# Attention and a feed-forward layer on one core: transposes, second products and the last output in another order

## The chip, the core and the metric

The kernel runs on one core of a Trainium2 chip. A core has five engines with instruction streams of their own: TensorE (PE in the profile; its weight loads are shown apart as PEld), VectorE (DVE), ScalarE (ACT), GpSimd (POOL) and SyncE (SP), which here only issues transfers. They wait for each other by semaphores. Transfers run on 16 DMA engines; what SP issues goes through a hardware queue, what GpSimd issues through a software queue. The metric is the time of one execution on the device, in microseconds (us); lower is better.

## The reference

Inputs are q, k, v of shape (4 batches, 8 heads, 768 positions, 64) in fp32, a decay lam for each head, and two weight matrices. Decayed linear attention comes first, then a feed-forward layer with an ELU:

```python
for b in range(nb):                     # blocks of 64 positions
    intra = np.einsum('bhic,bhjc->bhij', qb, kb) * Dmask[None]
    intra = np.einsum('bhij,bhjd->bhid', intra, vb)
    inter = np.einsum('bhid,bhde->bhie', qb * lam_pow[None], kv_state)
    out[:, :, sl] = intra + inter
    kv_state = lam_block[None, :, None, None] * kv_state + np.einsum('bhsd,bhse->bhde', kb_dec, vb)
...
h = x @ w_in                            # 3072 x 512 by 512 x 2048
g = np.where(h > 0.0, h, alpha * (np.exp(np.minimum(h, 0.0)) - 1.0))
return (g @ w_out).astype(np.float32)   # 3072 x 2048 by 2048 x 512
```

## The kernel before

The kernel takes blocks of 128 positions. Chunk g is one such block of one batch: batch g mod 4, block g div 4, 24 chunks in all. Every chunk goes through the attention and then through the feed-forward layer, and the stages of different chunks are interleaved by hand.

An order list of tokens is run one after the other; each token emits its instructions on all engines, and every engine keeps the order in which they were emitted. The first part of the list (`OPEN`, lines 51 to 59) is written by hand and reaches to the middle of chunk 6's and 7's second products; the rest is made by a rule (lines 575 to 612) that puts every other token at a fixed distance from the first products. The tokens are:

- `L12`: loads q, k, v of chunks 12 and 13 (three transfers that also cast to fp16, issued by GpSimd, line 107). From chunk 4 on chunks are loaded in pairs.
- `W9`: from chunk 8 on, issues the two transposing transfers of chunk 9 on SP (`qT`, `kT`, line 266), then on GpSimd `kd` = k times a decay (line 172) and the two products `stt` of the old state with the block's decay (line 376). The `stt` wait for the state of four chunks earlier. `T5` does the transposes of the first chunks on TensorE instead.
- `S8:9`: the score matmuls of chunks 8 and 9 on TensorE (line 300, into banks A, B and C, D of PSUM), and on VectorE four products `pp` with the causal mask (line 316); two of these at once, the others one by one with later tokens (the list `late`).
- `B:P8:P9:U8:U9`: the burst for both chunks: output of the attention (lines 336 and 342), its copy `xt` (line 359), and the new state (lines 404 and 416).
- `1:8:3`: part 3 of the first product for the pair that begins at chunk 8 (line 476, eight matmuls of 256 columns into one of the two buffers `psH`), then on ScalarE an exponential `e` (line 482) and a ReLU in place (line 483). VectorE's `g`, which combines them (line 455), is emitted with the next product token (`flush`), and only then is the `psH` buffer free.
- `2:6:3`: quarter 3 of the second product of chunk 6 (line 498, four matmuls of 512 columns that add to `psM`, of which there are two banks, M0 and M1). After quarter 3, ScalarE copies `psM` to `osb` (line 513; four buffers of 512 columns), and SP stores it (line 448); `mm1` emits all stores but the newest.

The last token is `2:23:3`, with `last` set: its four matmuls are done for columns 0 to 255 and again for 256 to 511, both in the same bank. VectorE copies the first half (line 511), ScalarE the second. `emit_stores` at the end emits what is left.

The part of the list that the change touches, with the rule's part behind the last line of `OPEN`:

```
S8:9 1:6:2 1:6:3 2:4:3 2:5:3 L12 1:6:4 B:P8:P9:U8:U9 1:6:5 W11 1:6:6 2:6:0 2:6:1 W10 1:6:7 2:6:2
1:8:0 S10:11 1:8:1 1:8:2 2:6:3 1:8:3 W12 2:7:0 1:8:4 B:P10:P11:U10:U11 2:7:1 1:8:5 W13 2:7:2 1:8:6
```

Of the kernel before, what the change touches and what calls it, by code (L numbers as in the profile page):

```python
# [7 lines left out]
FP32 = mybir.dt.float32  # L8
FP16 = mybir.dt.float16
# [6 lines left out]
def kernel(  # L16
# [11 lines left out]
    nc = tc.nc  # L28

    B, H, S, D = q.shape  # L30
    L = 128
    NHP = H // 2
    DM = H * D
    DFF = moe_w_in.shape[1]
    NFT = DFF // 128
    NCB = S // L
    NG = B * NCB
    FB = 4
    NJ = NFT // FB
    GPE = 8  # L40
    GSIZE = {**{g: 1 for g in range(4)}, **{g: 2 for g in range(4, NG, 2)}}
    GFIRST = {g0 + i: g0 for g0, n in GSIZE.items() for i in range(n)}
    WI = [2] * 8
# [15 lines left out]
    )  # L59
    LAGU = 7  # L60
    AT = {"L": -18, "W": -13, "T": -9, "S": -8, "B": -4}
# [10 lines left out]
    asb = ctx.enter_context(tc.tile_pool(name="asb", bufs=1))  # L72
    msb = ctx.enter_context(tc.tile_pool(name="msb", bufs=1))
    ps = ctx.enter_context(tc.tile_pool(name="ps", bufs=1, space=bass.MemoryType.PSUM))
# [45 lines left out]
    def cast_raw(g, w, eng):  # L120
        n = f"{w}{g}"
        t = asb.tile([128, 1, H, 64], FP16, tag=f"{w}n1", name=f"{w}n{g}", bufs=4)
        (qg if w == "q" else kg)[g] = t
        if eng == 0:
            nc.vector.tensor_copy(t[:, 0], raw[n][:])
        else:
            nc.scalar.copy(t[:, 0], raw[n][:])

    def of(tiles, g):
        g0, i = group_of[g]  # L130
        return tiles[g0][:, i]

    wi16, wo16, wi_of, wo_of = [], [], {}, {}
# [113 lines left out]
    def bank(what, i, shape, dtype, name):  # L247
        tag = TAGS[what].split()[i]
        return ps.tile(
            shape, dtype, tag=f"ps{tag}", name=name, bufs=2 if tag == "H" else 1  # L250
        )
# [10 lines left out]
    def att_T_dma(g):  # L262
        ts = []
        for w, tiles in (("q", qg), ("k", kg)):
            t = asb.tile([128, NHP, 128], FP16, tag=f"{w}T", name=f"{w}T{g}", bufs=5)
            nc.sync.dma_start_transpose(
                out=t[:], in_=of(tiles, g).rearrange("p h d -> p (h d)")
            )
            ts.append(t)
        qkT[g] = ts  # L270

    def att_T_pe(g):
        n = len(TAGS[f"T{g}"].split())
        pts = [
            bank(f"T{g}", i, [128, 2 // n, NHP, 128], FP16, f"psT{g}_{i}")
            for i in range(n)
        ]
        pts = [pts[0][:, 0], pts[n - 1][:, 2 // n - 1]]
        for src, pt in zip((of(qg, g), of(kg, g)), pts):
            for hp in range(NHP):  # L280
                nc.tensor.transpose(  # L281
                    pt[:, hp, :], in_=src[:, 2 * hp : 2 * hp + 2, :], identity=ident16[:]
                )
        qt, kt = [
            asb.tile([128, NHP, 128], FP16, tag=f"{w}T", name=f"{w}T{g}", bufs=5)
            for w in "qk"
        ]
        nc.vector.tensor_tensor(out=qt[:], in0=pts[0], in1=qs[:], op=ALU.mult)
        nc.scalar.copy(out=kt[:], in_=pts[1])
        qkT[g] = (qt, kt)  # L290
# [34 lines left out]
    def att_P(g):  # L325
# [21 lines left out]
        def evacuate():  # L347
            g0 = GFIRST[g]
            n = GSIZE[g0]
            if g0 not in xg:  # L350
# [4 lines left out]
            dst = xg[g0][:, :, (g - g0) * 128 : (g - g0 + 1) * 128]  # L355
            if g < GPE:
                nc.scalar.copy(out=dst, in_=po[:])  # L357
# [85 lines left out]
    gts, psM, stores, pending = {}, {}, [], []  # L443

    def emit_stores(keep=0):
        while len(stores) > keep:
            dst, o = stores.pop(0)
            nc.sync.dma_start(out=dst, in_=o)

    def flush():  # L450
        while pending:
            g0, j, e, r = pending.pop(0)
            n = GSIZE[g0]
            g = msb.tile([128, FB // n, n, 128], FP16, tag="g", bufs=40, name=f"g{g0}_{j}")
            nc.vector.scalar_tensor_tensor(  # L455
                out=g[:].rearrange("p f c t -> p (f c t)"), in0=e[:], scalar=-1.0, in1=r[:],
                op0=ALU.add, op1=ALU.min,
            )
            for f in range(FB // n):
                for c in range(n):  # L460
                    gts[(g0 + c, j * (FB // n) + f)] = g[:, f, c, :]
        if late:
            late.pop(0)()

    def mm1(g0, j):
        flush()
        emit_stores(1)
        n = GSIZE[g0]
        assert {f"P{g0 + i}" for i in range(n)} <= seen
# [15 lines left out]

    mm2_done = {g: 0 for g in range(NG)}

    def mm2(g, j, last=False):
        flush()
        if mm2_done[g] == 0:  # L490
            psM[g] = bank(f"M{g}", 0, [128, DM], FP32, f"psM{g}")
        first, mm2_done[g] = mm2_done[g] == 0, mm2_done[g] + 1
        end = mm2_done[g] == NJ
        halves = [slice(0, DM // 2), slice(DM // 2, DM)] if last else [slice(0, DM)]
        for hi, cols in enumerate(halves):
            for f in range(FB):
                i, w = wo_of[j * FB + f]
                nc.tensor.matmul(  # L498
                    psM[g][:, cols], lhsT=gts[(g, j * FB + f)], rhs=wo16[i][:, w, cols],
                    start=first and f == 0, stop=end and f == FB - 1, skip_group_check=True,  # L500
                )
            if end:
                out_of(g, cols, nc.vector if last and hi == 0 else nc.scalar)

    def out_of(g, cols, eng):
        cb, b = divmod(g, B)
        t0 = b * S + cb * L
        w = cols.stop - cols.start
        o = msb.tile([128, w], FP32, tag=f"osb{w}", bufs=4, name=f"osb{g}_{cols.start}")
        if eng is nc.vector:  # L510
            eng.tensor_copy(o[:], psM[g][:, cols])
        else:
            eng.copy(o[:], psM[g][:, cols])  # L513
        stores.append((out[t0 : t0 + 128, cols], o[:]))

    def zero_st(b):
        nc.scalar.memzero(st[b][0][:])
# [5 lines left out]
    def pool_work(g):  # L523
        if g >= GPE:
            att_T_dma(g)
        att_kd(g)
        att_M(g)
# [3 lines left out]
    def ready(t):  # L531

        g = int(t[1:])
        if t[0] == "P":
            assert g < B or f"U{g - B}" in seen
        if t[0] == "U" and g < 2 * B:
            assert f"{'z' if g < B else 'Z'}{g % B}" in seen
        if t[0] == "U" and g >= B:
            assert f"U{g - B}" in seen and (g < 2 * B or f"P{g - B}" in seen)
        seen.add(t)  # L540

    def run(t):
        w, *a = t[0], *t[1:].replace(":", " ").split()
        if w == "B":
            for o in a:
                ready(o)
            burst(*a)
            return
        a = [int(x) for x in a]
        if w in "PUzZ":  # L550
            ready(t)
        if w == "S":
            for g in a:
                att_S(g)
            for g in a:
                late.extend(att_E(g))
            late.pop(0)()
            late.pop(0)()
        elif w == "P":
            burst(t)  # L560
        elif w == "U":
            late.extend(att_U(*a))
            while late:
                late.pop(0)()
        else:
            {"T": att_T_pe, "1": mm1, "2": mm2, "Z": zero_st, "z": zero_st1,
             "q": lambda g, e: cast_raw(g, "q", e), "k": lambda g, e: cast_raw(g, "k", e),
             "c": lambda i: (emit_qs, emit_mask, emit_ks)[i](), "W": pool_work, "L": load_pair,
             "M": next_M, "w": zero_matmuls}[w](*a)

    for t in FIRST.split():
# [3 lines left out]
    prog = OPEN.split()  # L575
    done = set(prog) | {o for t in prog if t[0] == "B" for o in t.split(":")}
    m1 = [(g, j) for g, n in GSIZE.items() for j in range(NJ * n)]
    place = {u: i for i, u in enumerate(m1)}
    need = {
        (g, j): place[(GFIRST[g], ((j + 1) * FB - 1) // (FB // GSIZE[GFIRST[g]]))]  # L580
        for g in range(NG) for j in range(NJ)
# [3 lines left out]
    for g in range(0, NG, 2):  # L585
        u = place[(GFIRST[g], 0)] - (8 if GSIZE[GFIRST[g]] == 4 and g == GFIRST[g] else 0)
        for t, p in (
# [4 lines left out]
            h = int(t[1:].replace(":", " ").split()[0].strip("P"))  # L592
            if t[0] == "W" and h < 8 or t[0] == "L" and h < 12 or t[0] == "T" and h >= GPE or t in done:
                continue
# [4 lines left out]
    first = place[m1[0]]  # L599
# [10 lines left out]
            n -= 1  # L610
    for g, j in m2:
        prog.append(f"2:{g}:{j}")
    prog[-1] += ":1"
    for t in prog:
        run(t)
    while late:
        late.pop(0)()
    emit_stores()
# [30 lines left out]
```

## Time and profile before

| what | us |
|---|---|
| median of 3 runs | 216.61 |
| lowest and highest of the 3 | 215.79, 217.13 |
| the profiled execution, its own time | 217.26 |
| its span, first to last instruction | 215.5 |
| first products, L476: 896 matmuls, busy | 99.3 |
| second products, L498: 388 matmuls, busy | 96.4 |
| `g` on VectorE, L455: 96 of 0.686 | 65.8 |
| ScalarE's `e` and ReLU, L482 and L483: 96 each of about 0.6 | 57.3 and 57.0 |
| store of 256 KB (`out_dram<-osb`), issue to landing, median | 2.3 |
| transposes `qT` and `kT`, issue to landing, median | 3.9 and 2.8 |
| loads of q, k, v in pairs, issue to landing, median | 7.0, 8.3, 8.6 |

A row of the profile names the line and engine, the operation, what it writes and reads, the shape, the number of instructions, the busy time and the mean time of one; behind the bar or in square brackets stands the idle time of the engine just before, and what ended it. In a row of the order in time the first two numbers are the start from the span's beginning and the length. TensorE's granted clock was 0.997 of full speed on the mean. Because matmuls are pipelined, a group's shown length has its drain in it, and the next group can start before the shown end.

### The profile page before, as it was taken

How to read it: one execution, taken by the hardware profiler on the slowest of the kernel's cores; microseconds unless marked ns; L12 is line 12 of the kernel's file. 1: busy time of each engine (PE TensorE's matmuls, PEld its weight loads, DVE VectorE, ACT ScalarE, POOL GpSimd, SP SyncE). 2: the span in 40 equal slices, each digit the busy share in tenths (PEclk: the TensorE clock that was granted, in tenths of full speed). 3: DMA queues.
4: the chain of work that ended last, by engine and by line, in shares of the span. 5: the costliest groups of instructions: out<-in, count | busy, mean ns of one | idle time of the engine just before them, and what ended most of it. 6: DMA issues, size and time to landing. Idle time of an engine off the chain costs nothing.

```text
span 215.5 us, 5132 instructions
## 1 busy us (share of the span) xinstructions
PE 203.4 (94%) x2054; PEld 137.8 (64%) x2054; DVE 130.1 (60%) x224; ACT 129.1 (60%) x245; POOL 96.1 (45%) x115
## 2 busy tenths in 40 slices
PE   7767899999999998999999999999999999999992
PEld 2455577768685775766766766766766666766641
DVE  3936363787837788658657667667567456544410
ACT  4545565874776656565565566476476576566720
POOL 7996991999996419177167159300000000000000
PEclk9999999999999999999999999999999999999998
DMA  8999999999999957979939919999123110111021
GB/s 89 140 176 192 191 137 172 153 173 143 151 156 179 128 108 108 155 119 110 160 85 114 179 63 101 149 182 151 52 73 73 52 49 0 55 49 49 3 92 54
DMA packets 101977, 24.59 MB, mean 114 GB/s; under 512 B 92609, under 2 KB 99009, under 8 KB 101953
## 3 DMA queue, kind: packets, MB, share of 16 engines
q0 software_dynamic: 79760, 13.50, 83.1%
q1 hardware_dynamic: 22192, 10.76, 22.5%
q8 instruction: 16, 0.26, 0.5%
q14 instruction: 9, 0.07, 0.1%
HBM read 27.27 MB, written 6.29 MB: 156 GB/s over the span
## 4 chain that ended last, share of the span: by engine, by line
PE 83%; DMA 7%; POOL 6%; issue 1%; DVE 1%; ACT 0%; SPq 0%; POOLq 0%
PE psM L498 38%; PE psH L476 36%; DMA wo<-in_moe_w_out_dram 4%; DMA kT<-kn 3%; PE psO L336 3%; PE psS L300 3%; PE psO L342 2%; POOL wi L146 1%; POOL kn L107 1%; POOL vn L107 1%; POOL qn L107 1%; PE psT L281 1%; PE psU L404 1%; POOL kd L172 0%; POOL wo L153 0%
## 5 line engine op out<-in xcount | busy, mean ns | idle before, releaser
L476 PE MATMUL psH<-xt,wi 128*128 128x256 f16 (+1 forms) x896 | 99.3, 257 | 2.4 <-DMA wi<-in_moe_w_in_dram 0.9
L455 DVE SCALAR_TENSOR_TENSOR g<-e,psH 128x512 f16<-128x512 f32 x96 | 65.8, 686 | 57.6 <-ACT psH L483 56.8
L498 PE MATMUL psM<-wo,g 128*128 128x512 f16 (+1 forms) x388 | 96.4, 377 | 1.4 <-DMA wo<-in_moe_w_out_dram 0.9
L482 ACT ACTIVATE e<-psH 128x512 f32<-128x512 f32 x96 | 57.3, 597 | 66.4 <-PE psH L476 63.2
L476 PEld LDWEIGHTS <-wi 128*128 128x128 f16 x896 | 77.0, 98 | 27.7 <-DVE g L455 2.0
L483 ACT ACTIVATE psH<-psH 128x512 f32<-128x512 f32 x96 | 57.0, 594 | 0.0
L498 PEld LDWEIGHTS <-g 128*128 128x128 f16 x388 | 36.3, 98 | 30.4 <-issue 1.8
L316 DVE TENSOR_TENSOR pp<-psS,mask 128x512 f16<-128x512 f32 x48 | 30.9, 685 | 4.2 <-PE psS L300 4.2
L172 POOL TENSOR_TENSOR kd<-kn,ks 128x512 f16<-128x512 f16 x20 | 20.7, 1039 | 18.0 <-DMA kn<-in_k_dram 17.1
L376 POOL TENSOR_TENSOR stt<-st,upp 64x256 f32<-64x256 f16 x32 | 19.5, 608 | 19.2 <-DVE st L416 13.6
L513 ACT COPY osb<-psM 128x512 f32<-128x512 f32 (+1 forms) x24 | 13.9, 581 | 6.3 <-PE psM L498 6.3
L107 POOL DMA_DIRECT2D vn<-in_v_dram x14 | 15.5, 1109 | 1.9 <-DMA wi<-in_moe_w_in_dram 1.9
L107 POOL DMA_DIRECT2D kn<-in_k_dram x14 | 15.5, 1106 | 0.8 <-POOLq L633 0.8
L107 POOL DMA_DIRECT2D qn<-in_q_dram x13 | 14.8, 1139 | 0.0
L416 DVE TENSOR_TENSOR st<-stt,psU 64x256 f16<-64x256 f32 x32 | 13.3, 417 | 1.2 <-PE psU L404 0.5
L336 PE MATMUL psO<-pp,vn 128*64 128x128 f16 x192 | 12.0, 222 | 1.7 <-DMA vn<-in_v_dram 1.5
L359 DVE TENSOR_TENSOR xt<-psO,qs 128x512 f16<-128x512 f32 x16 | 11.0, 688 | 4.1 <-PE psO L342 4.1
L336 PEld LDWEIGHTS <-vn 128*64 128x64 f16 x192 | 9.7, 109 | 5.1 <-issue 2.9
L342 PE MATMUL psO<-qT,st 128*64 128x128 f16 x160 | 10.0, 219 | 0.0
L342 PEld LDWEIGHTS <-st 128*64 128x64 f16 x160 | 8.9, 110 | 0.0
L300 PE MATMUL psS<-qT,kT 64*128 64x128 f16 x192 | 8.1, 218 | 0.9 <-DMA kT<-kn 0.5
L357 ACT CAST xt<-psO 128x512 f16<-128x512 f32 x8 | 4.4, 588 | 6.9 <-PE psO L336 4.8
(41 smaller groups left out, 70.8 us busy)
## 6 DMA issues: line engine op xcount, KB each, us to landing
out_dram<-osb SPq DMA_DIRECT2D x23, 256.0 KB, 2.3
kn<-in_k_dram POOLq DMA_DIRECT2D x10, 256.0 KB, 8.3
qn<-in_q_dram POOLq DMA_DIRECT2D x10, 256.0 KB, 7.0
vn<-in_v_dram POOLq DMA_DIRECT2D x10, 256.0 KB, 8.6
wi<-in_moe_w_in_dram POOLq DMA_DIRECT2D x8, 256.0 KB, 6.9
wo<-in_moe_w_out_dram POOLq DMA_DIRECT2D x8, 256.0 KB, 7.9
kn<-in_k_dram POOLq DMA_DIRECT2D x4, 128.0 KB, 4.1
vn<-in_v_dram POOLq DMA_DIRECT2D x4, 128.0 KB, 5.9
```

The costliest lines, as they stand in the source:

```text
L107: nc.gpsimd.dma_start(out=t[:].rearrange("p b h d -> p (b h) d"), in_=src)
L172: nc.gpsimd.tensor_tensor(out=kd[:], in0=of(kg, g), in1=ks[:].unsqueeze(2).broadcast_to([128, H, 64]), op=ALU.mult,)
L300: nc.tensor.matmul(psS[g][hh][:, hp, :], lhsT=kt[r, hp, :], rhs=qt[r, hp, :], start=True, stop=True,)
L316: nc.vector.tensor_tensor(out=P[:], in0=pts[hh][:], in1=mask[:, hh::2, :], op=ALU.mult)
L336: nc.tensor.matmul(po[r, hp, :], lhsT=vt[:, 2 * hp + hh, :], rhs=Pt[(g, hh)][:, hp, :], start=True, stop=(cb == 0), skip_group_check=True,)
L342: nc.tensor.matmul(po[r, hp, :], lhsT=st[b][cb % 2][:, hp, r], rhs=qt[:, hp, :], start=False, stop=True, skip_group_check=True,)
L376: nc.gpsimd.tensor_tensor(out=tmp[r], in0=old[r, :, r], in1=upp[r].unsqueeze(2).broadcast_to([64, NHP, 64]), op=ALU.mult,)
L455: nc.vector.scalar_tensor_tensor(out=g[:].rearrange("p f c t -> p (f c t)"), in0=e[:], scalar=-1.0, in1=r[:], op0=ALU.add, op1=ALU.min,)
L476: nc.tensor.matmul(pH[:, f * n * 128 : (f + 1) * n * 128], lhsT=wi16[i][:, kk, w * 128 : (w + 1) * 128], rhs=xg[g0][:, kk, :], start=(kk = ...
L482: nc.scalar.activation(e[:], pH[:], AF.Exp)
L483: nc.scalar.activation(pH[:], pH[:], AF.Relu)
L498: nc.tensor.matmul(psM[g][:, cols], lhsT=gts[(g, j * FB + f)], rhs=wo16[i][:, w, cols], start=first and f == 0, stop=end and f == FB - 1, ...
```

## The change

A sixth buffer is given to `qT` and `kT`. In the hand-written list, `W11` and `W10` move ahead of `1:6:4` and `L12` moves behind `2:6:1`; the list goes on to `2:7:1`, with the second products `2:6:3`, `2:7:0` and `2:7:1` each placed ahead of `1:8:1`, `1:8:2` and `1:8:3`, and none of them between `1:8:3`, `1:8:4`, the burst of 10 and 11, and `1:8:5`. The last chunk's second product is made for columns 0 to 383 in its four tokens, and for columns 384 to 511 in a new function `mm2_rest` after them, in bank A. VectorE copies the first part, ScalarE the second, and each part's store is emitted at once.

```diff
+    LAST = NG - 1
+    CUT = 384
...
-        "2:4:2 S8:9 1:6:2 1:6:3 2:4:3 2:5:3 L12 1:6:4 B:P8:P9:U8:U9 1:6:5 W11 1:6:6 2:6:0 "
-        "2:6:1 W10 1:6:7 2:6:2"
+        "2:4:2 S8:9 1:6:2 1:6:3 2:4:3 2:5:3 W11 W10 1:6:4 B:P8:P9:U8:U9 1:6:5 1:6:6 2:6:0 "
+        "2:6:1 L12 1:6:7 2:6:2 1:8:0 S10:11 2:6:3 1:8:1 2:7:0 1:8:2 2:7:1"
...
-            t = asb.tile([128, NHP, 128], FP16, tag=f"{w}T", name=f"{w}T{g}", bufs=5)
+            t = asb.tile([128, NHP, 128], FP16, tag=f"{w}T", name=f"{w}T{g}", bufs=6)
...
-    def mm2(g, j, last=False):
+    def mm2(g, j):
         flush()
+        cols = slice(0, CUT if g == LAST else DM)
...
-        halves = [slice(0, DM // 2), slice(DM // 2, DM)] if last else [slice(0, DM)]
-        for hi, cols in enumerate(halves):
-            for f in range(FB):
-                i, w = wo_of[j * FB + f]
-                nc.tensor.matmul(
-                    psM[g][:, cols], lhsT=gts[(g, j * FB + f)], rhs=wo16[i][:, w, cols],
-                    start=first and f == 0, stop=end and f == FB - 1, skip_group_check=True,
-                )
-            if end:
-                out_of(g, cols, nc.vector if last and hi == 0 else nc.scalar)
+        for f in range(FB):
+            i, w = wo_of[j * FB + f]
+            nc.tensor.matmul(
+                psM[g][:, cols], lhsT=gts[(g, j * FB + f)], rhs=wo16[i][:, w, cols],
+                start=first and f == 0, stop=end and f == FB - 1, skip_group_check=True,
+            )
+        if end:
+            out_of(g, psM[g][:, cols], cols, nc.vector if g == LAST else nc.scalar)
+
+    def mm2_rest():
+        cols = slice(CUT, DM)
+        rest = ps.tile([128, DM - CUT], FP32, tag="psA", name="psMrest", bufs=1)
+        for f in range(NFT):
+            i, w = wo_of[f]
+            nc.tensor.matmul(
+                rest[:], lhsT=gts[(LAST, f)], rhs=wo16[i][:, w, cols],
+                start=f == 0, stop=f == NFT - 1,
+            )
+        out_of(LAST, rest[:], cols, nc.scalar)
...
         stores.append((out[t0 : t0 + 128, cols], o[:]))
+        if g == LAST:
+            emit_stores()
...
-    prog[-1] += ":1"
     for t in prog:
         run(t)
+    mm2_rest()
```

More of the change, by code (lines that the diff above doesn't have):

```diff
@@ L284, in att_T_pe @@
         qt, kt = [
-            asb.tile([128, NHP, 128], FP16, tag=f"{w}T", name=f"{w}T{g}", bufs=5)
+            asb.tile([128, NHP, 128], FP16, tag=f"{w}T", name=f"{w}T{g}", bufs=6)
             for w in "qk"
@@ L493, in mm2, with out_of @@
         end = mm2_done[g] == NJ
-        halves = [slice(0, DM // 2), slice(DM // 2, DM)] if last else [slice(0, DM)]
-        for hi, cols in enumerate(halves):
-            for f in range(FB):
-                i, w = wo_of[j * FB + f]
-                nc.tensor.matmul(
-                    psM[g][:, cols], lhsT=gts[(g, j * FB + f)], rhs=wo16[i][:, w, cols],
-                    start=first and f == 0, stop=end and f == FB - 1, skip_group_check=True,
-                )
-            if end:
-                out_of(g, cols, nc.vector if last and hi == 0 else nc.scalar)
-    def out_of(g, cols, eng):
+        for f in range(FB):
[16 more added lines that the diff above has]
+        out_of(LAST, rest[:], cols, nc.scalar)
+    def out_of(g, src, cols, eng):
         cb, b = divmod(g, B)
@@ L510, in out_of @@
         if eng is nc.vector:
-            eng.tensor_copy(o[:], psM[g][:, cols])
+            eng.tensor_copy(o[:], src)
         else:
-            eng.copy(o[:], psM[g][:, cols])
+            eng.copy(o[:], src)
         stores.append((out[t0 : t0 + 128, cols], o[:]))
+        if g == LAST:
+            emit_stores()
     def zero_st(b):
```

## The prediction

> **What bounds the kernel.** I read the page first, then busy time by stretches, then the order in time of TensorE, VectorE and the SP queue where TensorE stood still. The page:
>
> ```profile
> span 215.5 us, 5132 instructions
> ...
> PE 203.4 (94%) x2054; PEld 137.8 (64%) x2054; DVE 130.1 (60%) x224; ACT 129.1 (60%) x245; POOL 96.1 (45%) x115
> ...
> PE   7767899999999998999999999999999999999992
> ...
> PE 83%; DMA 7%; POOL 6%; issue 1%; DVE 1%; ACT 0%; SPq 0%; POOLq 0%
> ```
>
> TensorE is the bound. Its tenths are below 9 in the first five slices (before 27 us), in the one around 83 us, and at the end. The chain of waits adds a DMA share. An order change can win only where TensorE stands; the stretches say where that is past the start:
>
> ```profile
> 66.00:72.00 6.00, 5.49 (x56) 3.98 (x54) 5.16 (x10) 2.75 (x7) 4.24 (x7) 1.00 1.96 206
> ...
> 78.00:84.00 6.00, 5.74 (x52) 3.62 (x50) 5.06 (x10) 3.51 (x8) 3.95 (x6) 1.00 0.71 132
> 84.00:90.00 6.00, 5.49 (x72) 4.08 (x74) 3.98 (x7) 4.48 (x9) 2.93 (x3) 1.00 1.40 109
> ```
>
> The first number after the comma is TensorE's busy time of 6 us. All other stretches from 24 to 210 us show 6.00. A matmul's shown time has some 0.17 us of drain in it (4 of 256 columns take 0.60 us, but the next group starts 0.43 us on), so the true holes are that much larger than the idle shown. TensorE's order in time:
>
> ```profile
> 69.00 0.40 PE L300 MATMUL psS<-qT,kT 64*128 64x128 f16 x8
> 69.90 0.40 PE L300 MATMUL psS<-qT,kT 64*128 64x128 f16 x8 [0.51 <-DMA kT<-kn]
> 70.23 1.92 PE L476 MATMUL psH<-xt,wi 128*128 128x256 f16 x16
> ...
> 82.69 1.05 PE L476 MATMUL psH<-xt,wi 128*128 128x256 f16 x8
> 84.52 1.05 PE L476 MATMUL psH<-xt,wi 128*128 128x256 f16 x8 [0.77 <-DVE g L455]
> 85.40 1.03 PE L498 MATMUL psM<-wo,g 128*128 128x512 f16 x4
> ```
>
> Hole A is the score step S8:9. Both chunks' scores take 0.56 us elsewhere (97.28 to 97.84), here 1.23: **0.67 us** lost to the transposed k of chunk 9. Hole B lies between the first products 1:8:1 and 1:8:2. One takes 0.87 us, so the second was due at 83.56 and started at 84.52: **0.96 us** lost. VectorE shows why:
>
> ```profile
> 82.57 1.29 DVE L316 TENSOR_TENSOR pp<-psS,mask 128x512 f16<-128x512 f32 x2 [0.20 <-PE psS L300]
> 83.78 0.68 DVE L455 SCALAR_TENSOR_TENSOR g<-e,psH 128x512 f16<-128x512 f32 x1
> ```
>
> 1:8:2 needs the psH buffer of 1:8:0, whose g stands behind two score masks. Hole A on the SP queue:
>
> ```profile
> 61.60 1.22 SPq L266 DMA_TRANSPOSE qT<-qn  x1
> 62.86 1.31 SPq L266 DMA_TRANSPOSE kT<-kn  x1
> 64.27 10.07 SPq L448 DMA_DIRECT2D out_dram<-osb  x3
> ```
>
> The second is kT of chunk 9. It took 7.0 us to land (69.86), against a median of 2.8. The loads L12 (q, k, v of 12 and 13) were issued from GpSimd at 61.76, 62.96 and 64.09; before that, from 61.0 to 62.8, the software queue moved nothing. Hole C is the tail:
>
> ```profile
> 204.38 6.64 PE L498 MATMUL psM<-wo,g 128*128 128x512 f16 x32
> 211.06 0.42 DVE L511 COPY osb<-psM 128x256 f32<-128x256 f32 x1 [4.62 <-PE psM L498]
> 211.54 0.60 PE L498 MATMUL psM<-wo,g 128*128 128x256 f16 x4 [0.52 <-DVE osb L511]
> 212.18 0.37 ACT L513 COPY osb<-psM 128x256 f32<-128x256 f32 x1 [3.55 <-PE psM L498]
> ```
>
> 28 matmuls of 512 columns at 0.216 us and 4 of 256 at 0.108 end their issue at 210.85; the last 4 could follow, but wait for VectorE's read of the same bank until 211.54: **0.69 us**.
>
> **The change, part by part.** *L12 behind W11 and W10.* The loads now queue on GpSimd behind kd11, the two stt of 11, kd10 and the two stt of 10. The stt of 11 need chunk 7's state and start at 67.80 in the trace even now, so the order is: kd11 61.8, stt 67.80 to 69.1, kd10 1.0, stt 1.3, and q, k, v of L12 at about 71.5, 72.7, 73.9. That is some 10 us later, clear of kT9, which then has only its own queue's work before it. I take the row of T11 and T10, which land in 2.4 us with no load in flight; bound above by qT9's 4.4: landed at 65.3 to 67.3, needed at 69.2. Hole A goes: **-0.67**. If the cover fails, 0 is gained. Behind the L12 loads wait kd12, T12 and S12:13. With the latencies of before (q 6.6, k 8.3) they land at 78.1 and 81.0; four transposes at 1.3 each are issued by 86 and land, with the longest of before (6.6), by 92. S12:13 was at 97.28 and comes to about 96.0: 4 us of cover, so 0. GpSimd's L14 slips from 83.4 to about 85.4; T14 is not issued before 96, so 0.
>
> *T11, T10 ahead of two stores on SP.* Four issues, 5.2 us, pass the stores of chunks 3 and 4. Their osb buffers are wanted again only by the fourth copy after (chunk 7's, about 94 us), so 0; S10:11 did not wait for T10 even in the old order, so no gain either. The sixth qT/kT buffer takes away the wait for P8 that the earlier place would bring.
>
> *Second products between 1:8:x.* 2:6:3 now stands before 1:8:1, 2:7:0 before 1:8:2, 2:7:1 before 1:8:3. In times of the old trace (scores from 82.14): 2:6:3 at 82.69, 1:8:1 83.56, 2:7:0 84.43, 1:8:2 85.30. g of 1:8:0 ends at 84.47, so hole B goes: -0.96. ScalarE's copy of chunk 6 now comes before the exponential of 1:8:1; it fits (83.8 to 84.4, that product's exponential from 84.7). Next come 2:7:1 at 86.17, 1:8:3 87.03 and, as nothing stands between any more, 1:8:4 due at 87.90. It needs g of 1:8:2. In the undisturbed late stage a first product started at 200.04 has its g ended at 202.98, 2.94 us later; so 85.30 + 2.94 = 88.24, and with 0.05 us to the start as in hole B, 88.29: **+0.39**, a new wait. The burst takes 1.36 us after a first product (88.87 to 90.23), so 1:8:5 comes at 90.52, after g of 1:8:3 (89.97); 1:8:6 at 92.26, after g of 1:8:4 (91.3). Nothing else is late; 1:8:6 was at 92.84, which is **-0.57** in all (0.01 by rounding). Bounds of the new wait: 0 (VectorE's masks leave it free) to 0.96, that of hole B.
>
> *The last chunk.* 16 matmuls of 384 columns and 16 of 128 replace 12 of 512 and 8 of 256; columns are equal. A 128-column matmul with 128x128 weights runs at 0.056 us in this trace:
>
> ```profile
> 40.08 0.89 PE psH L476 x16
> ```
>
> So 0.89 us for 16, and 16 of 384 columns 2.57 (between the rows of 256 and 512): 3.46 us from 207.83, issue over at 211.29 instead of 211.98, **-0.69**. The second part has its own bank A, last read a stage earlier, and waits for nothing. The Trainium skill, page "TensorE: Matmul & The Clock Gate", section "Back-to-back issue gap", speaks against short matmuls: it gives about 81 ns for each at 128 columns in a stream with weight loads; an estimate by that is 1.30 us and a tail gain 0.41 us smaller. The row decides. ScalarE's last copy: 512 columns take 0.591, 256 take 0.372, so 128 about 0.26: **-0.11**. The last store shrinks from 128 to 64 KB: the last 256 KB landed in 2.0 us, both of 128 KB in 1.7; half the step again is **-0.15** (bounds 0 and -0.3). The first part's copy, about 0.53 by its 256-column row, ends near 211.2 and its store lands near 213.1, before the last (211.8 + 1.55).
>
> Sum: -0.67 - 0.57 - 0.69 - 0.11 - 0.15 = -2.19 us. The profiled execution took 217.26 us for a span of 215.5; it would take 215.1, span 213.3. The median of the runs is 216.61, 0.65 below it: **214.4**.
>
> **Rivals.** (1) kT9 stays late, because its delay is its own queue's (qT9 and a store in front) and T11, T10 follow close behind. For: qT9 took 4.4 us, issued just before the loads. Against: T11 and T10 landed in 2.4. 216.6 - 1.52 = 215.1. (2) The new wait before 1:8:4 is as long as the old, since first products 3 and 4 now stand together: 2.19 - 0.57 = 1.62, 215.0. (3) The second part does not run free: its weight loads (98 ns each in the trace) are not hidden, 16 x 0.098 = 1.57 instead of 0.89, and the tail gains 0.27: 215.1. Against it is the row of 0.89, with the same weights. (4) Slower: the delayed L12 loads come too late for S12:13. Cover 4 us plus the 2.2 won: it decides when they land over 6.2 us later than worked out. At double the longest v landing of before (9.5), 9.5 later, 9.5 - 6.2 = 3.3 lost: 219.9.
>
> **How the numbers follow.** Forecast 0.70, rivals 0.09, 0.09, 0.07 and 0.05. The forecast's own range: at best the new wait is 0 and the store gains 0.3 (214.4 - 0.54), at worst the store gains nothing, with 0.3 us either way for the medians (215.79 to 217.13 shown): 213.5 to 214.9. To 215.3 it takes in the first three rivals; 213.5 to 215.3. About 1% (2.17 us) is what a measurement of this kernel can tell from no change. The sum stands at that edge: 0.55 of the chance on faster by over 1%, nearly all in the forecast; 0.40 within 1%, with rivals 1 to 3; 0.05 slower.
>
> **What would show it.** Right: S8:9 in 0.56 us without a DMA wait; 1:8:2 without its hole and about 0.4 us before 1:8:4; in the tail no VectorE wait on TensorE and 32 matmuls in 3.46 us; S12:13 without a wait. Wrong: kT9 landing after 69 us, a hole before 1:8:5 or 1:8:6, gaps among the 128-column matmuls, or TensorE waiting for kT of 12 or 13 near 96 us.

## The result, and the profile after

| | before | after |
|---|---|---|
| median of nine runs, us | 217.13 (215.79 to 217.73) | 215.32 (214.60 to 215.71) |
| the profiled execution | 217.26 | 215.00 |
| its span | 215.5 | 213.2 |

The ratio is 0.9917, with a 95% interval from 0.9891 to 0.9943: faster by 0.8%, which is inside the 1% that the prediction called no change. The nine runs of the kernel before have a median 0.52 us above that of the first three. The profiled pair differs by 2.26 us, the medians by 1.81. The page of the changed kernel:

```profile
span 213.2 us, 5156 instructions
...
PE 202.7 (95%) x2066; PEld 138.1 (65%) x2066; DVE 130.1 (61%) x224; ACT 129.0 (61%) x245; POOL 96.2 (45%) x115
...
PE   7667999999999999999999999999999999999994
...
PE 82%; POOL 8%; DMA 7%; issue 1%; ACT 1%; DVE 0%; POOLq 0%; ACTq 0%
```

The slice around 83 us is full now; only the first four and the last are not. The chain still has 7% of transfers, but by its lines these are the first weights (4% and 3%); kT, which had 3% before, is gone from it. Some line numbers have moved: L302 is the scores, L478 the first and L499 the second product, L457 `g`, L484 and L485 the exponential and the ReLU, L450 the store, L268 the transposes, L511 the new second part of the last output, L523 and L525 its copies. The three stretches that had holes (the first number after the comma is TensorE's busy time of 6 us):

```profile
66.00:72.00 6.00, 6.00 (x58) 4.29 (x57) 5.17 (x10) 3.55 (x7) 4.13 (x6) 1.00 0.61 102
...
78.00:84.00 6.00, 6.00 (x54) 3.93 (x53) 5.28 (x11) 3.24 (x7) 3.37 (x5) 1.00 1.81 128
84.00:90.00 6.00, 5.78 (x82) 4.35 (x81) 3.73 (x7) 4.20 (x8) 4.52 (x5) 1.00 1.24 145
```

One hole is left, between 84 and 90 us. The order in time on TensorE:

```profile
68.83 0.62 PE L302 MATMUL psS<-qT,kT 64*128 64x128 f16 x16
69.39 1.92 PE L478 MATMUL psH<-xt,wi 128*128 128x256 f16 x16
...
82.72 1.04 PE L478 MATMUL psH<-xt,wi 128*128 128x256 f16 x8
83.60 1.03 PE L499 MATMUL psM<-wo,g 128*128 128x512 f16 x4
84.46 1.04 PE L478 MATMUL psH<-xt,wi 128*128 128x256 f16 x8
85.33 1.03 PE L499 MATMUL psM<-wo,g 128*128 128x512 f16 x4
86.20 1.04 PE L478 MATMUL psH<-xt,wi 128*128 128x256 f16 x8
87.45 1.03 PE L478 MATMUL psH<-xt,wi 128*128 128x256 f16 x8 [0.22 <-DVE g L457]
```

S8:9 takes 0.56 us (68.83 to 69.39) where it took 1.23. 1:8:2 (84.46) follows 1:8:1 after 1.74 us, with 2:7:0 between them and no hole. 1:8:4 was due 0.87 us after 86.20 and starts at 87.45: 0.38 us lost to `g` of 1:8:2, which VectorE's row shows:

```profile
86.71 0.69 DVE L457 SCALAR_TENSOR_TENSOR g<-e,psH 128x512 f16<-128x512 f32 x1 [1.05 <-ACT psH L485]
```

It ends at 87.40. On the SP queue, the first row is kT of chunk 9; one store follows, and then the transposes of 11 and 10, of which the third row is the first:

```profile
62.91 1.27 SPq L268 DMA_TRANSPOSE kT<-kn  x1
64.27 0.52 SPq L450 DMA_DIRECT2D out_dram<-osb  x1
64.98 1.23 SPq L268 DMA_TRANSPOSE qT<-qn  x1
```

The view of that tile gives its time from issue to landing, least, median and most of the one transfer:

```profile
DMA to landing us min/median/max: 2.5/2.5/2.5
```

It was 7.0 before. The tail:

```profile
202.97 6.22 PE L499 MATMUL psM<-wo,g 128*128 128x512 f16 x32
209.03 1.06 PE L511 MATMUL psMrest<-wo,g 128*128 128x128 f16 x16
209.23 0.56 DVE L523 COPY osb<-psM 128x384 f32<-128x384 f32 x1 [4.19 <-PE psM L499]
210.12 0.27 ACT L525 COPY osb<-psMrest 128x128 f32<-128x128 f32 x1 [2.91 <-PE psMrest L511]
```

VectorE's copy and TensorE's second part now run side by side. From the first of the last 32 matmuls to ScalarE's last copy it is 7.15 us (202.97 to 210.12); it was 7.80 (204.38 to 212.18). The 16 short matmuls take 1.06 us as shown, 0.89 without the drain.

### The profile page after: what moved, and what is told of

Read it like the earlier page. It is cut to its first block, busy times and chain, and to the rows that moved or that the text cites. A ratio compares the mean times of both kernels' runs of the same rounds, so it can differ in the third digit from the quotient of the medians.

```text
span 213.2 us, 5156 instructions
## 1 busy us (share of the span) xinstructions
PE 202.7 (95%) x2066; PEld 138.1 (65%) x2066; DVE 130.1 (61%) x224; ACT 129.0 (61%) x245; POOL 96.2 (45%) x115
## 4 chain that ended last, share of the span: by engine, by line
PE 82%; POOL 8%; DMA 7%; issue 1%; ACT 1%; DVE 0%; POOLq 0%; ACTq 0%
PE psM L499 36%; PE psH L478 35%; DMA wi<-in_moe_w_in_dram 4%; DMA wo<-in_moe_w_out_dram 3%; PE psO L338 3%; PE psS L302 3%; PE psO L344 2%; POOL kd L174 1%; POOL wi L148 1%; POOL kn L109 1%; POOL vn L109 1%; PE psU L406 1%; PE psT L283 1%; POOL qn L109 1%; POOL wo L155 1%
## 5 line engine op out<-in xcount | busy, mean ns | idle before, releaser
L478 PE MATMUL psH<-xt,wi 128*128 128x256 f16 (+1 forms) x896 | 99.3, 258 | 2.0 <-DMA wi<-in_moe_w_in_dram 1.1
L457 DVE SCALAR_TENSOR_TENSOR g<-e,psH 128x512 f16<-128x512 f32 x96 | 65.8, 686 | 56.7 <-ACT psH L485 56.0
L484 ACT ACTIVATE e<-psH 128x512 f32<-128x512 f32 x96 | 57.3, 597 | 65.0 <-PE psH L478 62.8
L499 PE MATMUL psM<-wo,g 128*128 128x512 f16 (+1 forms) x384 | 95.6, 377 | 0.7 <-DMA wo<-in_moe_w_out_dram 0.7
L478 PEld LDWEIGHTS <-wi 128*128 128x128 f16 x896 | 76.9, 98 | 27.4 <-DMA wi<-in_moe_w_in_dram 1.8
L485 ACT ACTIVATE psH<-psH 128x512 f32<-128x512 f32 x96 | 57.0, 593 | 0.0
L499 PEld LDWEIGHTS <-g 128*128 128x128 f16 x384 | 35.9, 98 | 29.3 <-issue 1.3
L525 ACT COPY osb<-psM 128x512 f32<-128x512 f32 x23 | 13.5, 590 | 3.2 <-PE psM L499 3.2
L302 PE MATMUL psS<-qT,kT 64*128 64x128 f16 x192 | 7.9, 218 | 0.3 <-ACT kT L291 0.3
```

Of the source, the lines that this page charges most:

```text
L302: nc.tensor.matmul(psS[g][hh][:, hp, :], lhsT=kt[r, hp, :], rhs=qt[r, hp, :], start=True, stop=True,)
L457: nc.vector.scalar_tensor_tensor(out=g[:].rearrange("p f c t -> p (f c t)"), in0=e[:], scalar=-1.0, in1=r[:], op0=ALU.add, op1=ALU.min,)
L478: nc.tensor.matmul(pH[:, f * n * 128 : (f + 1) * n * 128], lhsT=wi16[i][:, kk, w * 128 : (w + 1) * 128], rhs=xg[g0][:, kk, :], start=(kk = ...
L484: nc.scalar.activation(e[:], pH[:], AF.Exp)
L485: nc.scalar.activation(pH[:], pH[:], AF.Relu)
L499: nc.tensor.matmul(psM[g][:, cols], lhsT=gts[(g, j * FB + f)], rhs=wo16[i][:, w, cols], start=first and f == 0, stop=end and f == FB - 1, ...
```

## The experiments

All programs are the same up to about 60 us. So each profile is cut at the start of S8:9: what lies before is the scatter of the start, where TensorE waits for its first loads, and what lies after is the programs' difference. All times in us; hole A is what S8:9 takes beyond 0.56. Each ratio is to executions of the kernel before that ran beside that kernel, and their median moved too: 217.13 for the first changed row, 216.77 for "changed, again", old tail, loads first and old second products, 217.38 for "before, again", even second products, cut at 256 and old transposes, 217.09 for the other three. So a ratio is not the quotient of two medians of this table.

| kernel | start of S8:9 | from there to the end | kT9 to landing | hole A | median of its runs, ratio to before, interval |
|---|---|---|---|---|---|
| before | 69.00 | 146.5 | 7.0 | 0.67 | 217.13 |
| before, again | 69.43 | 145.8 | 5.9 | 0 | 217.12, 0.9984, 0.9952 to 1.0016 |
| before, third | 68.36 | 146.4 | 6.8 | 0.64 | 216.81, 0.9982, 0.9946 to 1.0019 |
| changed | 68.83 | 144.4 | 2.5 | 0 | 215.32, 0.9917, 0.9891 to 0.9943 |
| changed, again | 68.62 | 144.4 | 2.5 | 0 | 215.21, 0.9924, 0.9895 to 0.9954 |
| old tail | 69.59 | 145.2 | 2.5 | 0 | 216.24, 0.9982, 0.9954 to 1.001 |
| loads first | 69.04 | 144.6 | 6.5 | 0.20 | 215.59, 0.9956, 0.9928 to 0.9985 |
| old second products | 69.60 | 145.0 | 2.5 | 0 | 215.64, 0.9957, 0.9928 to 0.9986 |
| even second products | 69.00 | 144.1 | 2.5 | 0 | 215.03, 0.9897, 0.9855 to 0.9939 |
| the same, again | 69.69 | 144.1 | 2.5 | 0 | 214.88, 0.9902, 0.9869 to 0.9935 |
| cut at 256 | 69.32 | 144.6 | 2.5 | 0 | 215.15, 0.9905, 0.9869 to 0.9940 |
| old transposes | 69.57 | 148.7 | 2.5 | 0 | 218.33, 1.0051, 1.0018 to 1.0085 |
| five buffers | 68.70 | 144.4 | 2.5 | 0 | 214.94, 0.9891, 0.9845 to 0.9936 |

The first column moves by 1.3 us between executions (68.36 to 69.69), the second repeats to its last digit for the changed kernel. The medians have that scatter in them, so terms of some tenths are read from the second column.

**The changed kernel again.**

> The changed kernel once more, unedited, as the reference for the other experiments. Theory (every term of the sum has its size, and the medians differ from the one profiled pair by the scatter of the first 25 us, where TensorE waits for loads): from the start of the scores S8:9 (68.8 us) to the span's end 144.4 us as in its first profile (213.2 - 68.8), within 0.1, while the start of S8:9 itself moves by some tenths; ratio to the kernel before 0.990 to 0.993. Rival (the holes are smaller in most runs of the kernel before than in its one profile): the same stretch here, but the ratio to before nearer 0.995.

144.4 again, and a ratio of 0.9924, as the theory had it. The rival's ratio of 0.995 lies at the edge of the interval and isn't excluded by this run.

**The last output as before.** `mm2` and `out_of` of the kernel before, everything else changed:

```diff
-            out_of(g, psM[g][:, cols], cols, nc.vector if g == LAST else nc.scalar)
+                out_of(g, cols, nc.vector if last and hi == 0 else nc.scalar)
...
-    mm2_rest()
+    prog[-1] += ":1"
```

> The changed kernel with the last output as before (columns 0 to 255 and 256 to 511 of the last token in one bank). Theory: the wait of TensorE for VectorE's copy is back (0.69 us), ScalarE's last copy is 0.37 instead of 0.27 us and the last store 128 KB (0.1 us): 0.85 to 0.95 us more after the start of S8:9, so 145.3 us from there to the end; the middle is as in the changed kernel, with 0.38 us before 1:8:4. Rival (the short second part in its own bank pays for itself in another way, for example by weight loads that are not hidden): under 0.5 us more.

0.8 us more after S8:9, with the old wait back in TensorE's order:

```profile
210.89 0.60 PE L498 MATMUL psM<-wo,g 128*128 128x256 f16 x4 [0.52 <-DVE osb L511]
```

145.2 us for the 145.3 of the theory; its rival (under 0.5) falls.

**The loads first.**

```diff
-2:5:3 W11 W10 1:6:4 ... 2:6:1 L12 1:6:7
+2:5:3 L12 W11 W10 1:6:4 ... 2:6:1 1:6:7
```

> The changed kernel with the loads L12 ahead of W11 and W10, where they were before; the transposes of 11 and 10 stay ahead of the two stores. Theory (kT of chunk 9 is late because the loads of 12 and 13 share the DMA engines with it): it lands about 7 us after its issue, S8:9 takes 1.2 us instead of 0.56, 0.67 us more from S8:9 on, ratio to the changed kernel about 1.003. Rival 1 (its own queue makes it late: the queue's work is that of the changed kernel): 2.5 us to landing and no hole. Rival 2 (the late landing of the first profile was chance): landing between 3 and 6 us, no hole or a small one.

kT9 needs 6.5 us again, with SP's queue as in the changed kernel: the loads make it late, and not its own queue. But S8:9 took only 0.76 us:

```profile
69.04 0.83 PE L302 MATMUL psS<-qT,kT 64*128 64x128 f16 x16
69.80 1.92 PE L478 MATMUL psH<-xt,wi 128*128 128x256 f16 x16
```

So the cause is as the theory has it, and the price isn't: 0.20 instead of 0.67. TensorE came to the scores at nearly the same time as in the first profile of before (69.04 and 69.00), but the transfer landed earlier, at 62.92 + 6.5 = 69.42 instead of 69.86.

**The kernel before, two more profiles.**

> The kernel before once more, unedited, for a second profile. Theory: from the start of S8:9 to the span's end 146.5 us as in the first profile (215.5 - 69.0), within 0.1, with hole A of 0.67 us, hole B of 0.96 and the tail's 0.69; the start of S8:9 differs by some tenths. Rival (hole A depends on the run): kT of chunk 9 lands earlier than 7 us and hole A is under 0.4 us.

> The kernel before, unedited, for a third profile. Theory (hole A is what is left between the landing of kT9, 62.9 us plus 6 to 7, and the time at which TensorE comes to the scores of chunk 9, which moves by about 1 us with the start): kT9 lands 5.5 to 7.5 us after its issue; with S8:9 starting before 69.2 the hole is 0.2 to 0.9 us, with a start after 69.4 it is under 0.2. Rival (a fixed hole of 0.67 us): 0.6 to 0.7 whatever the start.

The scores in the second and the third profile:

```profile
69.43 0.62 PE L300 MATMUL psS<-qT,kT 64*128 64x128 f16 x16
```

```profile
68.36 0.40 PE L300 MATMUL psS<-qT,kT 64*128 64x128 f16 x8
69.23 0.40 PE L300 MATMUL psS<-qT,kT 64*128 64x128 f16 x8 [0.47 <-DMA kT<-kn]
```

Hole A is a race. In the second profile the transfer landed at 62.94 + 5.9 = 68.8, and TensorE came to chunk 9's scores at 69.66 (0.23 after the row's start): no hole. In the third it landed at 62.36 + 6.8 = 69.2, and TensorE was there at 68.6: 0.64. The first expectation's theory of a fixed hole fell, and its rival held; the second's theory, a race, held. Hole B (0.95 to 0.96) stood in all three.

**The second products as before.**

```diff
-1:6:7 2:6:2 1:8:0 S10:11 2:6:3 1:8:1 2:7:0 1:8:2 2:7:1
+1:6:7 2:6:2
```

> The changed kernel with the second products 2:6:3, 2:7:0 and 2:7:1 where they were before (behind 1:8:2, 1:8:3 and 1:8:4). Theory: the wait of 1:8:2 for g of 1:8:0 is back with 0.96 us, that of 1:8:4 (0.38 us) is gone: 0.57 us more from S10:11 to 1:8:6, ratio to the changed kernel about 1.0026. Rival (the masks of VectorE are earlier here, because the transposes are, and the old hole came from these): the hole at 1:8:2 stays away and the kernel is 0.38 us faster than the changed one.

```profile
82.61 1.05 PE L478 MATMUL psH<-xt,wi 128*128 128x256 f16 x8
84.43 1.05 PE L478 MATMUL psH<-xt,wi 128*128 128x256 f16 x8 [0.77 <-DVE g L457]
```

The hole of 0.96 us is back (84.43 instead of 83.48), the wait of 1:8:4 is gone, and 0.6 us more are needed after S8:9. So the order of the second products alone is worth 0.6.

**Second products evenly spread.** One place later, so that none is missing before 1:8:4:

```diff
-1:8:0 S10:11 2:6:3 1:8:1 2:7:0 1:8:2 2:7:1
+1:8:0 S10:11 1:8:1 2:6:3 1:8:2 2:7:0 1:8:3 W12 2:7:1
```

> The changed kernel with the same three second products one place later: 1:8:1 2:6:3 1:8:2 2:7:0 1:8:3 2:7:1 1:8:4, so that one stands between every two first products. Theory (a first product needs 2.94 us until its psH buffer is free, and two products in between cover it): 1:8:2 waits under 0.1 us for g of 1:8:0 (due 1.74 us after 1:8:1, g ready 1.8 us after it), 1:8:4 does not wait at all, 0.3 to 0.38 us less than the changed kernel, ratio to it about 0.9985. Rival (with S10:11 directly before 1:8:1 the masks delay g as in the kernel before, and a hole of 0.4 us or more stands at 1:8:2): no gain.

> The kernel with a second product between every two first products once more, for its time. Theory: from the start of S8:9 to the end 144.1 us as in its first profile (0.27 less than the changed kernel's 144.4); by the medians the two are not told apart, ratio to before 0.988 to 0.994. Rival (its gain is given back elsewhere in some runs): 144.4 or more.

```profile
82.02 1.05 PE L478 MATMUL psH<-xt,wi 128*128 128x256 f16 x8
...
83.84 1.05 PE L478 MATMUL psH<-xt,wi 128*128 128x256 f16 x8
...
85.58 1.04 PE L478 MATMUL psH<-xt,wi 128*128 128x256 f16 x8
...
87.32 1.04 PE L478 MATMUL psH<-xt,wi 128*128 128x256 f16 x8
```

The first products stand 1.82, 1.74 and 1.74 us apart: 0.09 us of hole B is left and no other wait. 144.1 in both profiles, 0.3 less than the changed kernel. By its two ratios it is the fastest form tried along with five buffers, but the medians do not tell it from the changed kernel.

**The last output cut at 256.** `CUT = 256`, still in two banks:

> The changed kernel with the last output cut at column 256 instead of 384, still in two banks. Theory: TensorE ends at the same time; ScalarE's last copy takes 0.37 instead of 0.27 us and the last store of 128 KB lands in 1.7 instead of 1.6 us: 0.1 to 0.2 us more, so nearly all of the tail's gain is the second bank, not the short second part. Rival (the short part is what gains): 0.4 us or more.

0.2 us more (144.6). Of the 0.8 us of the tail the second bank, with the order of matmuls and the early store that go with it, brings 0.6, the short second part 0.2.

**The transposes at their old places.** L12 stays late, and `qT` and `kT` have five buffers again, as before the change (by itself that is worth nothing, as the last experiment shows):

```diff
-2:5:3 W11 W10 1:6:4 B:P8:P9:U8:U9 1:6:5 1:6:6 2:6:0 2:6:1 L12 1:6:7
+2:5:3 1:6:4 B:P8:P9:U8:U9 1:6:5 W11 1:6:6 2:6:0 2:6:1 W10 L12 1:6:7
```

> The changed kernel with W11 and W10 at their places of before, behind 1:6:5 and 2:6:1, and five buffers for qT and kT again; L12 stays late, behind W10. Theory (the earlier transposes are worth nothing by themselves; S10:11 does not wait for them): same as the changed kernel within 0.1 us from S8:9 on, S10:11 at the same distance from S8:9 (12.5 us). Rival (the early transposes carry the gain, or keep the SP queue free for the stores): S10:11 late, a wait on kT of 10 or 11, 0.3 us or more lost.

The expectation failed by 4.3 us. TensorE at S10:11, and the time to landing (least, median, most) of kT11 and kT10:

```profile
81.06 1.04 PE L478 MATMUL psH<-xt,wi 128*128 128x256 f16 x8
84.73 0.77 PE L302 MATMUL psS<-qT,kT 64*128 64x128 f16 x16 [2.63 <-DMA kT<-kn]
85.44 1.89 PE L499 MATMUL psM<-wo,g 128*128 128x512 f16 x4
87.12 1.71 PE L478 MATMUL psH<-xt,wi 128*128 128x256 f16 x8
```

```profile
DMA to landing us min/median/max: 5.2/6.6/8.0
```

At these places kT11 and kT10 landed in 2.4 and 2.5 us in the kernel before, when the loads were already there. Now the loads are issued at 72 to 75.5, and the transposes, issued from 74.4 to 79.5, run into them: the collision of chunk 9's transposes has become that of 10's and 11's. The scores were due at 82.03 and start at 84.73, 2.70 us late. The rest of the loss is the clock. In the view by stretches the number before the last two is the granted clock:

```profile
84.00:85.00 1.00, 0.27 (x10) 0.27 (x12) 0.00 (x0) 0.00 (x0) 1.00 (x2) 1.00 1.09 341
85.00:86.00 1.00, 1.00 (x16) 0.52 (x11) 0.83 (x2) 0.00 (x0) 0.93 (x3) 0.53 1.28 282
86.00:87.00 1.00, 1.00 (x4) 0.30 (x2) 1.00 (x3) 0.00 (x0) 1.00 (x1) 0.50 0.48 103
87.00:88.00 1.00, 1.00 (x6) 0.64 (x5) 1.00 (x3) 0.59 (x1) 1.00 (x2) 0.50 2.10 77
88.00:89.00 1.00, 1.00 (x7) 0.71 (x6) 0.25 (x1) 0.08 (x1) 1.00 (x2) 0.76 1.89 91
```

From about 85 to 88.5 us TensorE has half its clock, and from the scores to 1:8:2 4.79 us pass (84.73 to 89.52) instead of 3.16 (81.30 to 84.46 in the changed kernel): 1.63 us. With the 2.70 that is 4.33, as the table has it (148.7 less 144.4). The median of its twelve runs is 3.1 us above the changed kernel's, so this profile, the slowest of them, shows more than the usual loss.

**Five buffers.**

```diff
-name=f"{w}T{g}", bufs=6)
+name=f"{w}T{g}", bufs=5)
```

> The changed kernel with five buffers for qT and kT, as before the change; all else as changed. Theory (what the early place gives is that the transposes of 11 and 10 are done before the loads L12 are in flight, as the loss of the old places with late loads showed): qT of chunk 10 waits on SP for the buffer that the burst of chunk 8 frees (about 74.6 us), kT10 is issued near 76 us with the loads in flight, lands 5 to 8 us later (81 to 84 us) where S10:11 wants it at 81.4: a wait of 0 to 2.6 us on TensorE, and where it is over 2 us, a stretch of halved TensorE clock behind it with 1 to 2 us more. Rival (the sixth buffer is worth nothing): kT10 lands in 2.5 us, no wait, ratio as the changed kernel.

The theory fell and the rival held. T10's two transposes are issued at once after T11's:

```profile
67.14 1.21 SPq L268 DMA_TRANSPOSE qT<-qn  x1
68.44 1.22 SPq L268 DMA_TRANSPOSE kT<-kn  x1
```

They do not wait for the burst of chunk 8. 144.4 as in the changed kernel: the sixth buffer is worth nothing, and the early place was free to be had without it.

## Why the prediction was right or wrong

The measured time of 215.32 us lies just outside the range (213.5 to 215.3), and the gain was 1.81 instead of 2.19 us. The terms that the forecast added up were all there, each with its cause. What failed was two numbers: the start of the sum and the size of hole A; two remarks on terms put at 0 were wrong as well. Between the sum (216.61 - 2.19 = 214.42) and the measurement lie 0.90 us: 0.52 from the start, 0.38 from the gain. That the profiled pair met the forecast so well (2.26 us) was in part luck: the one profile of before had a full hole A, and another execution of it had none.

- *The start of the sum, "the median of the runs is 216.61".* It failed. Nine runs gave 217.13. The range allowed 0.3 us for both medians; this one moved by 0.52. Three runs that spread over 1.34 us did not fix a median to 0.3 us. 217.13 - 2.19 is 214.94.
- *"Hole A goes: -0.67."* The mechanism was right: kT9 lands in 2.5 us without the loads beside it (in all nine profiles with late loads) and in 5.9 to 7.0 with them. The size was that of one execution. In three profiles of the kernel before it was 0.67, 0 and 0.64, on the mean 0.44: 0.23 of the missing 0.38 us. The bound that was drawn for this term (0 if the cover fails) was on the side of after; the scatter was on the side of before. From S8:9 to the end the three profiles of before have a mean of 146.2 against 144.4, that is 1.8 us, as the medians show. Three profiles give this mean only roughly.
- *Second products, -0.57 with a new wait of 0.39.* Right: 1:8:6 came at 91.43 instead of 92.84, 1.41 us earlier, of which 0.84 us were there already at S10:11; so 0.57. The new wait was 0.38. Undoing this part cost 0.6.
- *The tail, -0.69 - 0.11 - 0.15.* TensorE's part was 0.65, the copy 0.27 instead of 0.37, the landing of the last store 1.6 instead of 1.7: 0.85 in all instead of 0.95, and 0.8 by the experiment; that is 0.10 of the missing 0.38. The measured terms, 0.44 + 0.57 + 0.85, add up to 1.86 us, against 1.81 by the medians. The row of 0.056 us for a short matmul held. The Trainium skill's 81 ns, from "TensorE: Matmul & The Clock Gate", section "Back-to-back issue gap", did not show in this stream: 16 matmuls took 0.89 us.
- *L12 later, 0; S12:13 without a wait.* Right: S12:13 started at 95.87 us (forecast about 96.0), and TensorE waits for nothing after 1:8:4.
- *T11 and T10 earlier: "no gain either".* Right for the place of the loads of before, wrong as a statement on the change: with the loads late, the old places cost 3 us by the medians. The two moves are one edit, and the step looked at each with the other left as it was.
- *"The sixth qT/kT buffer takes away the wait for P8."* Wrong: there is no such wait with five.

Rival 1 was settled by the loads-first experiment (not its own queue), rival 3 by the tail's rows, rival 4 by TensorE's rows after 90 us. Rival 2, a new wait as long as the old, did not come: 0.38 us, not 0.96.

## What to carry to other kernels

A hole at the end of a transfer is a race between its landing and the engine's arrival; both scatter, so its size is taken from several executions, or with 0 as its lower bound on the side of before too. A transfer that is moved out of one collision is to be followed to where it lands: here late loads were only good because the transposes had been moved ahead of them. And where two buffers feed a chain of 2.94 us with steps of 0.87, one filler step between every two is what keeps TensorE going; three fillers early and none later moved the hole and left 0.38 of its 0.96 us.

## What was not expected of the hardware

A hole of 2.70 us in TensorE's work (old transposes) was followed by half the granted clock (0.50 to 0.53) from about 85 to 88.5 us and cost another 1.63 us. Holes of up to 0.96 us in the same stage of the kernel before were not: its clock stays at 1.00 in those stretches. The Trainium skill, page "TensorE: Matmul & The Clock Gate", section "What's actually happening", has the clock halved after an idle window of about 3.4 us and given back after as long a busy one. The return fits; the hole here was shorter than that window.

The start of the profiles shows that the length of a hole alone does not decide. TensorE waits there once for a load of v. Its row, and the granted clock in 40 slices of the span, in the second profile of the kernel before:

```profile
12.38 0.64 PE L336 MATMUL psO<-pp,vn 128*64 128x128 f16 x16 [1.61 <-DMA vn<-in_v_dram]
PEclk9979999999999999999999999999999999999999
```

and in the second profile of the even second products:

```profile
12.91 0.64 PE L338 MATMUL psO<-pp,vn 128*64 128x128 f16 x16 [2.14 <-DMA vn<-in_v_dram]
PEclk9999999999999999999999999999999999999999
```

The wait of 1.61 us was followed by half the clock (0.50 from 14 to 16 us), the wait of 2.14 us was not. In the thirteen profiles this wait is 1.0 to 2.3 us long; six of them, from 1.61 us up, have half the clock after it. What decides besides the length no run here shows.
